# Rounding and splitting the second MoE's weights late, straight into their tiles, instead of early through a DRAM copy

## The chip, the cores and the metric

The program runs on one core of a Trainium2 chip. The metric is device time in microseconds (us) of one execution. The core's engines each take their own instructions strictly in order and wait for one another through semaphores: PE (TensorE, matmuls; PEld are its weight loads), DVE (VectorE), ACT (ScalarE), POOL (GpSimd) and SP (SyncE, which here issues every DMA).

## The reference, cut to what matters

```python
for t in range(768):                       # attention: a recurrence over tokens, 4 batches x 8 heads
    y_t = r_t . state                      # state is 40 x 40 for each head
    state = state * w_t - outer(state . a_t, b_t) + outer(v_t, k_t)
x = y as [3072 tokens, 320]
g = max(x @ moe_w_in, 0) ** 2              # first MoE, d_ff = 2048
x2 = g @ moe_w_out
out = ((x2 @ w_a) * (x2 @ w_b)) @ w_out2   # second MoE, d_ff = 1536
```

The inputs come as 64-bit floats (two 32-bit halves, low and high). The kernel has to round every weight to a 32-bit float, and then split it into a high part (type fp32r, which the matmuls take) and a low part (what is left), since the products are computed as high x high + low x high + high x low.

## The kernel before, in words

Attention runs in 24 waves of 32 tokens (`attention_moe`, loop over `w`). While PE works on a wave, `fill` and `stream.emit` put matmuls of the first MoE between the small attention matmuls. A unit is four waves, 512 tokens; `stream.add(g)` queues unit g of the first MoE one unit behind attention, so the last unit's products stand alone behind the last wave. A unit has 16 hidden blocks of 128; each is eight matmuls into `h` (`l1`), then relu and two squares on ACT (`Moe.l1`), the low part `gl` on DVE (`Moe.low`), and eight matmuls into the accumulators `x0` to `x2` (`l2`). Eleven of the sixteen blocks' weights are streamed from DRAM for every unit (`Stream.load`, double-buffered tiles `w0`, `w1`), five stay resident.

Weights are decoded by `Weights`, a pipeline of four steps for a piece of 384 or 320 columns: `load` (a DMA of 64-bit values into one of three `raw` buffers), `first` (one DVE and two ACT instructions), `second` (two DVE instructions, then an add on POOL that gives the rounded values in `dy`), and `put`, which differs from user to user. For the first MoE `put` splits them: a cast on ACT and a subtraction on POOL. One call of `weights.step()` advances all four steps by one piece.

The second MoE has 12 hidden blocks f, each with 1088 columns of weights (three pieces). In the kernel before, its 36 pieces are decoded by `decode` during the waves, as soon as the first MoE's weights are done; their `put` is a DMA of `dy` to the DRAM tile `w2s`. Behind the last wave, in the loop `while stream.parts`, `load_w2` reads each block back (`w2f`) and splits it by a cast on ACT (`w2h`) and a subtraction on DVE (`w2l`).

The second MoE (`l3`, `l4`) takes unit after unit: 16 matmuls into `h` and `b`, a copy `a` on ACT, the product on DVE, the cast `gh` on ACT, `gl` on DVE, and 12 matmuls into `o`. During its first blocks `General.range_ops` compares all decays w with limits on POOL (`w_t`, `w_ok`), 16 chunks, one for each block; then `in_range` reduces the result on DVE (`w_oks`) and adds it up with one small matmul. `General.run` is a slow fallback for inputs outside the limits, behind a branch that these inputs do not take.

What order each engine gets is decided when the program is built: the scheduler orders DVE, ACT, POOL and SP by a model of time, PE inside the waves keeps the written order, and `keep_in_program_order` (`pin`) holds some instructions in the written order.

Of the kernel before, what the change touches and what calls it, by code (L numbers as in the profile page):

```python
# [9 lines left out]
F32 = mybir.dt.float32  # L10
F32R = mybir.dt.float32r
# [3 lines left out]
ALU = mybir.AluOpType  # L15
# [9 lines left out]
DW = 384  # L25
# [7 lines left out]
RATE = 66  # L33
AHEAD = 3
KEEP = 24

WARM = 10
CHUNK = 4
# [23 lines left out]
class Attention:  # L62
# [51 lines left out]
    def warm(s, bank):  # L114

        x = s.idn.bitcast(BF16)
        for _ in range(WARM):
            s.nc.tensor.matmul(bank[:, 0:256], lhsT=x[:, 0:128], rhs=x, start=True, stop=True)
# [312 lines left out]
class Moe:  # L431
# [109 lines left out]
                s.nc.vector.tensor_tensor(out=x, in0=acc[i][0:64], in1=x, op=ALU.add)  # L541
                s.nc.sync.dma_start(out=dst[256:320], in_=x)

    def load_w2(s, pool, src, f):

        x = pool.tile([128, 1088], F32, tag="w2f", name="w2f", bufs=3)
        s.nc.sync.dma_start(out=x, in_=src)

        def split():
            hi = pool.tile([128, 1088], F32R, tag=f"w2h{f}", name="w2h")  # L550
            lo = pool.tile([128, 1088], F32R, tag=f"w2l{f}", name="w2l")
            pin = s.tc.keep_in_program_order
            pin(s.nc.scalar.copy(out=hi, in_=x))
            pin(s.nc.vector.tensor_tensor(out=lo, in0=x, in1=hi.bitcast(F32), op=ALU.subtract))
            s.w2[f] = hi, lo

        return split

    def l3(s, f, x, ps2, sb):
        hi, lo = s.w2[f]  # L560
# [109 lines left out]
class General:  # L670
# [2 lines left out]

    LEAST, MOST = 0.6, 1.6

    def __init__(s, tc, nat, wm1, w2s, xf, out):
        s.tc, s.nc, s.nat, s.wm1, s.w2s, s.xf, s.out = tc, tc.nc, nat, wm1, w2s, xf, out

    def range_ops(s, sb, n=480):

# [28 lines left out]

    def run(s):  # L710
        tc, nc = s.tc, s.nc
        nf1, nf2 = s.wm1.shape[0], len(s.w2s)
        with ExitStack() as c:
            sb = c.enter_context(tc.tile_pool(name="gen", bufs=1))
            two = c.enter_context(tc.tile_pool(name="gen2", bufs=2))
            ps = c.enter_context(tc.tile_pool(name="gen_ps", bufs=1, space=PSUM))
            weights = Weights(tc, sb)
            w1 = sb.tile([128, nf1, 704], F32, name="w1")
            w2 = sb.tile([128, nf2, 1088], F32, name="w2")
            for f in range(nf2):  # L720
                nc.sync.dma_start(out=w2[:, f], in_=s.w2s[f])
            for f in range(nf1):
                for o in range(0, 704, 176):
                    weights.add(s.wm1[f, :, o:o + 176], 176, lambda x, w=w1[:, f, o:o + 176]: nc.vector.tensor_copy(w, x))
            while weights.busy():
                weights.step()
            S = sb.tile([32, D, D], F32, name="S")
            nc.vector.memset(S, 0.0)
            idn = sb.tile([128, 128], F32, name="idn")
            make_identity(nc, idn)  # L730
            with tc.For_i(0, s.out.shape[0], 1) as i:
                names = "rkvwab"
                x = sb.tile([32, 6, TW, D], F32, name="x")
                for j, m in enumerate(names):
                    nc.sync.dma_start(
                        out=x[:, j].rearrange("p t d -> p (t d)"), in_=s.nat[m][:, bass.ds(i * (TW * D), TW * D)]
                    )
                y = sb.tile([32, TW, D], F32, name="y")
                for t in range(TW):
                    s.token(two, S, {m: x[:, j, t] for j, m in enumerate(names)}, y[:, t])  # L740
                h = sb.tile([40, 8, 4, TW], F32, name="h")
                for q in range(2):
                    p = ps.tile([128, 512], F32, tag="p", name="p", bufs=2)
                    for t in range(16):
                        nc.tensor.matmul(
                            p[0:40, 32 * t:32 * t + 32], lhsT=y[:, 16 * q + t], rhs=idn[0:32, 0:32], start=True, stop=True
                        )
                    for e in range(8):
                        nc.vector.tensor_copy(
                            h[:, e, :, 16 * q:16 * q + 16],  # L750
                            p[0:40].rearrange("p (t b e) -> p e b t", b=4, e=8)[:, e],
                        )
# [63 lines left out]
def attention_moe(ctx, tc, wakb, rv, vt, wm1, wm2, nat, out):  # L816
    nc = tc.nc
    n_waves = wakb.shape[0]
    n_groups = n_waves // GW
    nf1, nf2 = wm1.shape[0], wm2.shape[1]  # L820

    dram = ctx.enter_context(tc.tile_pool(name="dram", bufs=1, space=bass.MemoryType.DRAM))
# [6 lines left out]
    xf = dram.tile([320, 128], F32, name="xf")  # L829
    w1s = {  # L830
        f: [dram.tile([128, n], F32, name=f"w1s{f}_{n}") for n in (768, 640)] for f in range(nf1) if f not in RESIDENT
    }
    w2s = [dram.tile([128, 1088], F32, name=f"w2s{f}") for f in range(nf2)]

    def pool(c, name, side, bufs=1):
        return c.enter_context(tc.tile_pool(name=name, bufs=bufs, side=side, reuse_waits="tile"))
# [18 lines left out]
    done = set()  # L855
# [20 lines left out]

    wp = []
    pending = deque(stream.moving + list(RESIDENT))
    w2_pieces = deque()
    for f in range(nf2):  # L880
        o = 0
        while o < 1088:
            n = min(DW, 1088 - o)
            w2_pieces.append((f, o, n))
            o += n

    def decode(n):
        for _ in range(n):
            if not weights.queue:
                if pending:  # L890
                    round_block(pending.popleft())
                elif w2_pieces and len(done) == nf1:
                    f, o, m = w2_pieces.popleft()
                    weights.add(
                        wm2[:, f, o:o + m], m, lambda x, f=f, c=slice(o, o + m): nc.sync.dma_start(out=w2s[f][:, c], in_=x)
                    )
            if weights.busy():
                weights.step()

# [43 lines left out]
    if True:  # L943
# [51 lines left out]
        for w in range(n_waves):  # L995
          with tc.manual_schedule(engines=MAN):
# [66 lines left out]
              at.m_y(w)  # L1063
              prep(9)
              warm()
        stream.add(n_units - 1)
        stream.tick = lambda x: None
        while weights.busy() or w2_pieces:
            decode(1)
            stream.emit(1)  # L1070
        c1.close()

        w2p = pool(c3, "w2p", "left")
        def load_x2(g):
            h = xp.tile([128, 5, TOK], F32R, tag="xhl", name="xhl", bufs=2)[:, :, 0:x2s[g].shape[1]]
            return h, moe.load_x(h, x2s[g])

        splits = deque(moe.load_w2(w2p, w2s[f], f) for f in range(3))
        f = 3
        every = stream.left // (nf2 + 2)  # L1080
        x = None
        while stream.parts:
            stream.emit(every)
            if splits:
                splits.popleft()()
            if f < nf2:
                splits.append(moe.load_w2(w2p, w2s[f], f))
                f += 1
            elif x is None:
                x, split = load_x2(0)  # L1090
                splits.append(split)
        c2.close()
        ca.close()

        xp3 = pool(cb, "xp3", "right", 2)
        ps2 = psum(cb, "ps2", 2)
        acc4 = psum(cb, "acc4", 1)
        general = General(tc, nat, wm1, w2s, xf, out)
        ranges = general.range_ops(xp3)

        todo = n_ok = None
        for g in range(n_units):
            acc = None
            for f in range(nf2):
                if ranges:
                    ranges.popleft()()
                elif n_ok is None:
                    n_ok = general.in_range(xp3, ps2)
                c = moe.l3(f, x, ps2, xp3)
                if todo:  # L1110
                    todo()
                if f == 0:
                    acc = [acc4.tile([128, TOK], F32, tag=f"o{j}", name=f"o{j}") for j in range(UNITS[g])]
                if f == 3 and g + 1 < n_units:
                    x_next, split = load_x2(g + 1)
                if f == nf2 - 3 and g + 1 < n_units:
                    split()

                def todo(g=g, f=f, acc=acc, c=c):
                    moe.l4(f, c, acc, f == 0, f == nf2 - 1)  # L1120
                    if f == nf2 - 1:
                        for j in range(UNITS[g]):
                            moe.put_out(xp3, g, j, acc)

            if g + 1 < n_units:
                x = x_next
# [64 lines left out]
```

## Time and profile before

| | |
|---|---|
| median of 3 runs | 1320.24 us (1318.36 to 1321.07) |
| the profiled execution | 1315.96 us, its span 1314.2 us |
| PE busy | 1165.1 us, 89% of the span |
| DVE, ACT, POOL busy | 742.4, 520.6, 360.8 us |
| DMA | 153.26 MB, mean 117 GB/s |

The span is the time from the first to the last instruction. The last attention results (`Y`) are written at 825.3 us; the last unit of the first MoE runs until about 902 us, and the rest is the second MoE. In the rows below, "[3.38 <-DVE RVR L317]" behind an instruction is how long its engine was idle before it, and who released it; "x8" means eight instructions merged into one row. Lines are those of the kernel before.

### The profile page before, as it was taken

The numbers are of one execution on the slowest core, as the hardware profiler recorded it, in microseconds if no ns is written. First come the engines' busy times: TensorE is split into PE (matmuls) and PEld (weight loads), VectorE is DVE, ScalarE is ACT, GpSimd is POOL, SyncE is SP. The second block draws the span as 40 slices with busy tenths as digits, with TensorE's granted clock in tenths as the row PEclk, the third lists the DMA queues.
The fourth block names the chain that finished last, engine by engine and source line by source line (L and its number), as shares of the span: only waits on it lengthen the run. The fifth ranks groups of instructions, "written<-read, shape, count | busy, mean of one in ns | idle before, by whom it ended". The sixth has DMA issues, their size and how long they took to land.

```text
span 1314.2 us, 34391 instructions
## 1 busy us (share of the span) xinstructions
PE 1165.1 (89%) x14378; PEld 939.4 (71%) x14378; DVE 742.4 (56%) x1491; ACT 520.6 (40%) x1121; POOL 360.8 (27%) x502
## 2 busy tenths in 40 slices
PE   2537865799799989998999999999998999999997
PEld 2526754577577767776677777778887888888886
DVE  5986897758876886689569623443231323232222
ACT  2215533454455445545454444664221222222221
POOL 2475672324132422142224100001995000000000
PEclk9997677899989989999899999999998999999999
DMA  6307754453567456745753533773120101010000
GB/s 158 91 13 229 223 190 144 116 157 91 156 193 208 110 169 168 229 117 164 202 160 104 139 105 85 263 256 110 43 89 16 45 1 37 0 37 1 20 1 22
DMA packets 103483, 153.26 MB, mean 117 GB/s; under 512 B 40840, under 2 KB 61320, under 8 KB 101256
## 3 DMA queue, kind: packets, MB, share of 16 engines
q1 hardware_dynamic: 103320, 150.98, 39.5%
q8 instruction: 115, 1.88, 0.6%
q14 instruction: 48, 0.39, 0.1%
HBM read 121.38 MB, written 26.41 MB: 112 GB/s over the span
## 4 chain that ended last, share of the span: by engine, by line
PE 56%; DVE 21%; DMA 9%; POOL 8%; issue 4%; ACT 1%; SPq 1%; DVEq 0%; POOLq 0%; ACTq 0%
PE h L440 18%; PE a L108 13%; PE x L440 10%; PE b L440 8%; PE o L440 7%; DVE tmp L246 4%; DVE Ball L253 4%; POOL w_t L691 3%; DMA inp<-wakb 3%; POOL w_ok L692 3%; DVE KA L218 2%; DVE RVR L317 1%; DVE KA L189 1%; DMA xhl<-xs 1%; DVE W L166 1%
## 5 line engine op out<-in xcount | busy, mean ns | idle before, releaser
L440 PE MATMUL h<-xhl,w 128*128 128x512 f32 x768 | 230.9, 421 | 3.6 <-DVE xhl L443 2.6
L569 DVE TENSOR_TENSOR b<-b,a 128x512 f32<-128x512 f32 x72 | 50.3, 699 | 213.3 <-PE b L440 199.0
L440 PEld LDWEIGHTS h<-xhl,w 128*128 128x128 f32 x768 | 140.7, 194 | 36.8 <-DVE xhl L443 3.3
L440 PE MATMUL x<-gh,w 128*128 128x512 f32 x480 | 147.3, 420 | 1.0 <-DVE xl L541 0.6
L108 PE MATMUL a<-KA,KBT 40*64 40x80 f32 x1536 | 84.7, 269 | 56.7 <-POOL KBT L192 26.4
L440 PE MATMUL h<-xhl,w2h 128*128 128x512 f32 x360 | 127.8, 396 | 0.0
L108 PEld LDWEIGHTS a<-KA,KBT 40*64 40x64 f32 x1536 | 74.0, 163 | 74.8 <-POOL KBT L192 38.1
L443 DVE TENSOR_TENSOR gl<-h,gh 128x512 fp32r<-128x512 f32 x96 | 66.1, 689 | 103.7 <-ACT h L507 102.9
L425 POOL TENSOR_TENSOR dy<-dy,raw 128x384 int32<-128x384 int32 (+1 forms) x68 | 68.3, 1004 | 204.6 <-DVE dy L422 109.4
L440 PE MATMUL b<-xhl,w2h 128*128 128x512 f32 x360 | 120.4, 400 | 0.0
L505 ACT ACTIVATE h<-h 128x512 f32<-128x512 f32 x96 | 55.9, 582 | 132.6 <-PE h L440 130.8
L571 ACT CAST gh<-b 128x512 fp32r<-128x512 f32 x72 | 42.3, 587 | 161.9 <-DVE b L569 161.9
L440 PEld LDWEIGHTS x<-gh,w 128*128 128x128 f32 x480 | 89.4, 195 | 22.3 <-issue 1.3
L440 PE MATMUL x<-gl,w 128*128 128x512 f32 x288 | 92.7, 415 | 0.0
L566 ACT COPY a<-h 128x512 f32<-128x512 f32 x72 | 42.3, 588 | 121.9 <-PE h L440 121.9
L440 PE MATMUL h<-xhl,w2l 128*128 128x512 f32 x216 | 85.9, 397 | 0.0
L440 PE MATMUL b<-xhl,w2l 128*128 128x512 f32 x216 | 85.8, 397 | 0.0
L440 PE MATMUL o<-w2h,gl 128*128 128x320 f32 x288 | 85.6, 309 | 0.0
L440 PE MATMUL o<-w2l,gh 128*128 128x320 f32 x288 | 85.6, 308 | 0.0
L108 PEld LDWEIGHTS a<-RVR,VUT 40*64 40x64 f32 x1536 | 64.2, 144 | 24.8 <-issue 14.7
L440 PEld LDWEIGHTS b<-xhl,w2h 128*128 128x128 f32 x360 | 67.9, 190 | 15.8
L108 PE MATMUL a<-RVR,VUT 40*64 40x80 f32 x1536 | 74.6, 246 | 4.8 <-ACT KBS L216 2.4
(97 smaller groups left out, 2174.6 us busy)
## 6 DMA issues: line engine op xcount, KB each, us to landing
w<-w1s SPq DMA_DIRECT2D x66, 384.0 KB
w<-w1s SPq DMA_DIRECT2D x66, 320.0 KB
inp<-wakb SPq DMA_DIRECT2D x48, 322.7 KB
raw<-wm SPq DMA_DIRECT2D x40, 384.0 KB
raw<-wm SPq DMA_DIRECT2D x28, 320.0 KB
w2f<-w2s SPq DMA_DIRECT2D x12, 544.0 KB
w2s<-dy SPq DMA_DIRECT2D x24, 192.0 KB
w1s<-w SPq DMA_DIRECT2D x11, 384.0 KB
```

The lines of the kernel that those rows point to most:

```text
L108: s.nc.tensor.matmul(out, lhsT=lhsT, rhs=rhs, start=True, stop=True)
L246: engine.tensor_tensor(out=t, in0=s.BH[:, i + 1:TW, i:i + 1].to_broadcast([128, n, m]), in1=s.N[:, i:i + 1, c0:c1].to_broadcast([128, n, m ...
L253: engine.tensor_tensor(out=out, in0=out, in1=t, op=ALU.subtract)
L425: nc.gpsimd.tensor_tensor(out=yi, in0=yi, in1=low, op=ALU.add)
L440: s.nc.tensor.matmul(out, lhsT=lhsT, rhs=rhs, start=start, stop=stop)
L443: (engine or s.nc.vector).tensor_tensor(out=out, in0=x, in1=hi.bitcast(F32), op=ALU.subtract)
L505: s.nc.scalar.activation(out=ps, in_=ps, func=ACTF.Relu)
L566: s.nc.scalar.copy(out=a, in_=pa)
L569: s.nc.vector.tensor_tensor(out=pb, in0=pb, in1=a, op=ALU.mult)
L571: s.nc.scalar.copy(out=ch, in_=pb)
L691: nc.gpsimd.tensor_scalar(out=t, in0=x, scalar1=lim, scalar2=None, op0=op)
L692: nc.gpsimd.tensor_tensor(out=s.ok, in0=s.ok, in1=t, op=ALU.mult)
```

## The change

The 36 pieces of the second MoE's weights are no longer decoded during the waves, and there is no DRAM copy of them. All are queued behind the last wave. In the loop over the last unit's products, one `weights.step()` follows every eight matmuls (`W2_EVERY`), and `put` now casts `dy` on ACT and subtracts on POOL straight into the tiles `w2h` and `w2l`. What is left is stepped in the second MoE's first unit. In the source the load of x2's first unit stands where fewer than 16 products are left, and the chunks of the range check begin when no weights are pending. The fallback, which is not executed, decodes the weights itself.

```diff
+W2_EVERY = 8
-    def load_w2(s, pool, src, f):
-
-        x = pool.tile([128, 1088], F32, tag="w2f", name="w2f", bufs=3)
-        s.nc.sync.dma_start(out=x, in_=src)
-
-        def split():
-            hi = pool.tile([128, 1088], F32R, tag=f"w2h{f}", name="w2h")
-            lo = pool.tile([128, 1088], F32R, tag=f"w2l{f}", name="w2l")
-            pin = s.tc.keep_in_program_order
-            pin(s.nc.scalar.copy(out=hi, in_=x))
-            pin(s.nc.vector.tensor_tensor(out=lo, in0=x, in1=hi.bitcast(F32), op=ALU.subtract))
...
+    def add_w2(s, pool, weights, src, f):
...
+        def put(x, o):
+            if not tiles:
+                tiles.extend(pool.tile([128, n], F32R, tag=f"w2{t}{f}", name=f"w2{t}") for t in "hl")
+            hi, lo = (t[:, o:o + x.shape[1]] for t in tiles)
+            s.tc.keep_in_program_order(s.nc.scalar.copy(out=hi, in_=x))
+            s.low(lo, x, hi, weights.engine)
+            if o + x.shape[1] == n:
+                s.w2[f] = tiles
+
+        for o in range(0, n, DW):
+            m = min(DW, n - o)
+            weights.add(src[:, o:o + m], m, lambda x, o=o: put(x, o))
...
-                elif w2_pieces and len(done) == nf1:
-                    f, o, m = w2_pieces.popleft()
-                    weights.add(
-                        wm2[:, f, o:o + m], m, lambda x, f=f, c=slice(o, o + m): nc.sync.dma_start(out=w2s[f][:, c], in_=x)
-                    )
...
-        splits = deque(moe.load_w2(w2p, w2s[f], f) for f in range(3))
-        f = 3
-        every = stream.left // (nf2 + 2)
-        x = None
+        for f in range(nf2):
+            moe.add_w2(w2p, weights, wm2[:, f], f)
         while stream.parts:
-            stream.emit(every)
-            if splits:
-                splits.popleft()()
-            if f < nf2:
-                splits.append(moe.load_w2(w2p, w2s[f], f))
-                f += 1
-            elif x is None:
+            stream.emit(W2_EVERY)
+            weights.step()
+            if stream.left < 16 and x is None:
                 x, split = load_x2(0)
-                splits.append(split)
+        split()
...
+        w2_ready(1)
...
-                if ranges:
+                if ranges and not weights.busy():
                     ranges.popleft()()
-                elif n_ok is None:
+                elif not ranges and n_ok is None:
                     n_ok = general.in_range(xp3, ps2)
+                for _ in range(3 if weights.busy() else 0):
+                    weights.step()
+                w2_ready(f)
```

How the instructions now stand is read from the built programs. On ACT, in the middle of the last unit of the first MoE, before: one hidden block is the three ACTIVATE rows on `h` and `gh` (relu and two squares), and the casts to `w2h` stand between blocks.

```order
L505 ACTIVATE h<-h 128x512
L506 ACTIVATE gh<-h 128x512
L507 ACTIVATE h<-h 128x512
L553 CAST w2h<-w2f 128x1088
L505 ACTIVATE h<-h 128x512
L506 ACTIVATE gh<-h 128x512
L507 ACTIVATE h<-h 128x512
L553 CAST w2h<-w2f 128x1088
```

The same place on ACT now; `raw` and `dz` are the two ACT instructions of the decode step `first`, the cast to `w2h` belongs to `put`:

```order
L507 ACTIVATE h<-h 128x512
L418 ACTIVATE dz<-raw 128x384
L508 ACTIVATE gh<-h 128x512
L509 ACTIVATE h<-h 128x512
L555 CAST w2h<-dy 128x320
L414 ACTIVATE raw<-raw 128x384
L418 ACTIVATE dz<-raw 128x384
L507 ACTIVATE h<-h 128x512
L555 CAST w2h<-dy 128x384
L508 ACTIVATE gh<-h 128x512
L509 ACTIVATE h<-h 128x512
```

Decode instructions have moved in between the three instructions of a block. In the steady part of this stretch 17 casts stand in 12 blocks; 29 of the 36 casts stand ahead of the first `a` copy of the second MoE.

On POOL, from the last attention instruction (`VS`) on, before: one leftover piece, then the range check.

```order
L338 TENSOR_TENSOR VS_149<-VS_149,W_130 40x640 x2
L425 TENSOR_TENSOR dy<-dy,raw 128x320
L685 MEMSET w_ok 128x480
L691 TENSOR_SCALAR w_t<-w_all 128x480
L692 TENSOR_TENSOR w_ok<-w_ok,w_t 128x480
```

On POOL now, in the middle of the last unit: the add that ends the rounding (`dy`) and the subtraction of `put` (`w2l`).

```order
L445 TENSOR_TENSOR w2l<-dy,w2h 128x384
L427 TENSOR_TENSOR dy<-dy,raw 128x320
L427 TENSOR_TENSOR dy<-dy,raw 128x384
L445 TENSOR_TENSOR w2l<-dy,w2h 128x320
L445 TENSOR_TENSOR w2l<-dy,w2h 128x384
L427 TENSOR_TENSOR dy<-dy,raw 128x384
L445 TENSOR_TENSOR w2l<-dy,w2h 128x384
```

POOL, which had nothing between the last wave and the range check, now has 36 adds and 36 subtractions there, the last of them among the first chunks of the range check.

On ACT at the start of the second MoE, before: `a` and `gh` are the second MoE's own, the copies to `xl` and casts to `xhl` belong to x2.

```order
L566 COPY a<-h 128x512 x2
L540 COPY xl<-x_11291 64x512
L477 CAST xhl<-xl 128x512
L571 CAST gh<-b 128x512
```

The same place now:

```order
L571 COPY a<-h 128x512
L418 ACTIVATE dz<-raw 128x384
L555 CAST w2h<-dy 128x320
L414 ACTIVATE raw<-raw 128x384
L542 COPY xl<-x_10964 64x512
L418 ACTIVATE dz<-raw 128x384
L555 CAST w2h<-dy 128x384
L414 ACTIVATE raw<-raw 128x320
L479 CAST xhl<-xl 128x512
L418 ACTIVATE dz<-raw 128x320
L555 CAST w2h<-dy 128x384
L414 ACTIVATE raw<-raw 128x384
```

Nine decode instructions now stand between the second `a` copy and the first `gh` cast. PE's order is the same as before but for a few matmuls of the last unit and of the second MoE's first units that change places with a neighbour.

## Rows read from the trace of the kernel before

**Rows 1.** Busy time by stretch: us, then each engine's busy us, clock, DMA share, GB/s

```profile
338.40:469.30 130.90, 122.89 (x2068) 92.49 (x2069) 98.10 (x218) 67.59 (x153) 38.96 (x61) 0.96 0.58 165
469.30:598.60 129.30, 121.97 (x2042) 92.58 (x2041) 99.33 (x222) 64.02 (x148) 39.25 (x62) 0.96 0.61 171
598.60:729.40 130.80, 121.43 (x2074) 91.85 (x2074) 98.70 (x213) 67.09 (x154) 39.58 (x62) 0.97 0.56 159
...
827.50:902.10 74.60, 72.34 (x309) 57.03 (x308) 33.02 (x38) 48.92 (x80) 0.50 (x1) 1.00 0.71 238
```

**Rows 2.** Timeline of two waits of PE in the waves: start, us, engine, instruction

```profile
359.23 1.26 DVE L166 TENSOR_TENSOR_SCAN W<-inp,ini 104x528 f32<-104x528 f32 x1 [4.26 <-DMA inp<-wakb]
...
361.58 0.80 PE L108 MATMUL a<-KA,KBT 40*64 40x80 f32 x8 [3.38 <-DVE RVR L317]
...
638.98 0.56 DVE L422 SCALAR_TENSOR_TENSOR dy<-dz,dy 128x384 int32<-128x384 int32 x1
639.46 0.35 DVE L411 TENSOR_SCALAR dy<-raw 128x384 int32<-128x384 int32 x1
...
640.70 0.56 PE L108 MATMUL a<-VS,KA 96*32 96x40 f32 x20 [2.80 <-DVE KA L218]
```

**Rows 3.** Instructions of tiles dy and dz: count, duration ns least/median/most, first and last start

```profile
L411 DVE TENSOR_SCALAR dy<-raw x68: 311/353/1442, 91.6 to 694.0; 128x384 int32<-128x384 int32 x40, 128x320 int32<-128x320 int32 x28
L421 DVE TENSOR_SCALAR dz<-dz x68: 272/353/1147, 31.9 to 734.0; 128x384 f32<-128x384 f32 x40, 128x320 f32<-128x320 f32 x28
L422 DVE SCALAR_TENSOR_TENSOR dy<-dz,dy x68: 466/557/1411, 92.0 to 734.3; 128x384 int32<-128x384 int32 x40, 128x320 int32<-128x320 int32 x28
L425 POOL TENSOR_TENSOR dy<-dy,raw x68: 867/1012/2067, 92.7 to 735.0; 128x384 int32<-128x384 int32 x40, 128x320 int32<-128x320 int32 x28
```

**Rows 4.** Groups by line and shape: count, busy us, mean ns, idle before

```profile
L443 POOL TENSOR_TENSOR w<-dy,w 128x384 fp32r<-128x384 f32 x16 | 17.3, 1080 | 14.9 <-ACT w L450 14.8
L553 ACT CAST w2h<-w2f 128x1088 fp32r<-128x1088 f32 x12 | 13.1, 1092 | 0.0
L450 ACT CAST w<-dy 128x384 fp32r<-128x384 f32 x16 | 8.2, 510 | 2.5 <-POOL dy L425 2.4
```

**Rows 5.** Timeline: DVE beside POOL, at 607 us and at 985 us

```profile
607.16 1.26 POOL L186 TENSOR_TENSOR KBT<-inp,KBS 104x512 f32<-104x512 f32 x1 [10.50 <-DVE KBS L176]
607.29 1.35 DVE L411 TENSOR_SCALAR dy<-raw 128x384 int32<-128x384 int32 x1
...
984.64 1.41 POOL L691 TENSOR_SCALAR w_t<-w_all 128x480 f32<-128x480 f32 x1
984.67 0.69 DVE L443 TENSOR_TENSOR gl<-b,gh 128x512 fp32r<-128x512 f32 x1 [0.65 <-ACT gh L571]
```

**Rows 6.** Timeline of ACT: a decode pair in the waves, a hidden block in the last unit

```profile
633.39 0.54 ACT L412 ACTIVATE raw<-raw 128x384 f32<-128x384 uint32 x1
633.82 0.55 ACT L416 ACTIVATE dz<-raw 128x384 f32<-128x384 f32 x1
...
889.56 0.58 ACT L505 ACTIVATE h<-h 128x512 f32<-128x512 f32 x1 [0.98 <-PE h L440]
...
890.67 0.59 ACT L507 ACTIVATE h<-h 128x512 f32<-128x512 f32 x1
```

**Rows 7.** The chain that ended last: start, us, what

```profile
629.67 6.25 DMA inp<-wakb
...
867.33 1.87 PE x L440 x8
869.19 1.83 PE h L440 x8
```

**Rows 8.** Timeline of ACT at the second MoE's start: two rows

```profile
908.13 0.59 ACT L566 COPY a<-h 128x512 f32<-128x512 f32 x1 [0.77 <-PE h L440]
...
914.46 0.59 ACT L571 CAST gh<-b 128x512 fp32r<-128x512 f32 x1 [1.52 <-DVE b L569]
```

**Rows 9.** Waits of PE from 880 to 1060 us: total, times, longest

```profile
PE b L705 <- DVE w_oks L701: 5.2, 1, 5.2
```

**Rows 10.** Busy time by stretch, early waves, columns as in Rows 1

```profile
100.00:200.00 100.00, 75.69 (x1594) 63.79 (x1594) 86.37 (x175) 47.30 (x113) 66.76 (x100) 0.74 0.68 213
```

More of the change, by code (lines that the diff above doesn't have):

```diff
@@ L542, in put_x2 @@
                 s.nc.sync.dma_start(out=dst[256:320], in_=x)
-    def load_w2(s, pool, src, f):
-        x = pool.tile([128, 1088], F32, tag="w2f", name="w2f", bufs=3)
-        s.nc.sync.dma_start(out=x, in_=src)
-        def split():
-            hi = pool.tile([128, 1088], F32R, tag=f"w2h{f}", name="w2h")
-            lo = pool.tile([128, 1088], F32R, tag=f"w2l{f}", name="w2l")
-            pin = s.tc.keep_in_program_order
-            pin(s.nc.scalar.copy(out=hi, in_=x))
-            pin(s.nc.vector.tensor_tensor(out=lo, in0=x, in1=hi.bitcast(F32), op=ALU.subtract))
-            s.w2[f] = hi, lo
-        return split
+    def add_w2(s, pool, weights, src, f):
+        n = src.shape[1]
+        tiles = []
+        def put(x, o):
[9 more added lines that the diff above has]
+            weights.add(src[:, o:o + m], m, lambda x, o=o: put(x, o))
     def l3(s, f, x, ps2, sb):
@@ L674, with __init__ @@
     LEAST, MOST = 0.6, 1.6
-    def __init__(s, tc, nat, wm1, w2s, xf, out):
-        s.tc, s.nc, s.nat, s.wm1, s.w2s, s.xf, s.out = tc, tc.nc, nat, wm1, w2s, xf, out
+    def __init__(s, tc, nat, wm1, wm2, xf, out):
+        s.tc, s.nc, s.nat, s.wm1, s.wm2, s.xf, s.out = tc, tc.nc, nat, wm1, wm2, xf, out
     def range_ops(s, sb, n=480):
@@ L711, in run @@
         tc, nc = s.tc, s.nc
-        nf1, nf2 = s.wm1.shape[0], len(s.w2s)
+        nf1, nf2 = s.wm1.shape[0], s.wm2.shape[1]
         with ExitStack() as c:
@@ L719, in run @@
             w2 = sb.tile([128, nf2, 1088], F32, name="w2")
[L720 to L724, printed above, removed]
+            for m, src in [(w1[:, f], s.wm1[f]) for f in range(nf1)] + [(w2[:, f], s.wm2[:, f]) for f in range(nf2)]:
+                for o in range(0, m.shape[1], 176):
+                    w = m[:, o:min(o + 176, m.shape[1])]
+                    weights.add(src[:, o:o + w.shape[1]], w.shape[1], lambda x, w=w: nc.vector.tensor_copy(w, x))
             while weights.busy():
@@ L832, in attention_moe @@
     }
-    w2s = [dram.tile([128, 1088], F32, name=f"w2s{f}") for f in range(nf2)]
     def pool(c, name, side, bufs=1):
@@ L878, in attention_moe @@
     pending = deque(stream.moving + list(RESIDENT))
[L879 to L885, printed above, removed]
     def decode(n):
@@ L1065, in attention_moe @@
               warm()
+        x = None
         stream.add(n_units - 1)
         stream.tick = lambda x: None
-        while weights.busy() or w2_pieces:
+        while weights.busy():
             decode(1)
@@ L1076, in load_x2, with w2_ready @@
             return h, moe.load_x(h, x2s[g])
-        splits = deque(moe.load_w2(w2p, w2s[f], f) for f in range(3))
-        f = 3
-        every = stream.left // (nf2 + 2)
-        x = None
+        for f in range(nf2):
+            moe.add_w2(w2p, weights, wm2[:, f], f)
         while stream.parts:
-            stream.emit(every)
-            if splits:
-                splits.popleft()()
-            if f < nf2:
-                splits.append(moe.load_w2(w2p, w2s[f], f))
-                f += 1
-            elif x is None:
+            stream.emit(W2_EVERY)
+            weights.step()
+            if stream.left < 16 and x is None:
                 x, split = load_x2(0)
-                splits.append(split)
+        split()
         c2.close()
         ca.close()
+        def w2_ready(f):
+            while f < nf2 and f not in moe.w2:
+                weights.step()
+        w2_ready(1)
         xp3 = pool(cb, "xp3", "right", 2)
@@ L1097, in attention_moe @@
         acc4 = psum(cb, "acc4", 1)
-        general = General(tc, nat, wm1, w2s, xf, out)
+        general = General(tc, nat, wm1, wm2, xf, out)
         ranges = general.range_ops(xp3)
@@ L1104, in attention_moe @@
             for f in range(nf2):
-                if ranges:
+                if ranges and not weights.busy():
                     ranges.popleft()()
-                elif n_ok is None:
+                elif not ranges and n_ok is None:
                     n_ok = general.in_range(xp3, ps2)
+                for _ in range(3 if weights.busy() else 0):
+                    weights.step()
+                w2_ready(f)
                 c = moe.l3(f, x, ps2, xp3)
```

## The prediction

> **What bounds the kernel now.** I read the busy time by stretch first. In the three groups of four waves between 338 and 729 us PE is busy 122.9 of 130.9, 122.0 of 129.3 and 121.4 of 130.8 us, at a mean granted clock of 0.96 to 0.97; in the stretch of the first MoE's last unit, 827.5 to 902.1 us, it is busy 72.3 of 74.6 us at full clock [rows 1]. So PE bounds both, and each has little to give. What differs is who else is busy: DVE has 98 of 131 us in a group of waves, but 33 of 74.6 us in the last unit, where POOL has 0.5 us and ACT 48.9 [rows 1]. The change takes work from the stretch where DVE is nearly full to one where there seems to be room.
>
> Next the timeline around the waits that PE has in the waves. Two of the longest are 3.38 us at 361.6 and 2.80 us at 640.7, both for DVE [rows 2]. In the first, DVE itself had waited 4.26 us for a DMA (`inp`); in the second, 0.56 and 0.35 us of second-MoE decoding stand directly ahead of the instruction that PE wants. Then the durations of the decode instructions [rows 3, 4], what DVE does while POOL works [rows 5], the period of a hidden block [rows 6, 7], and the second MoE's start [rows 8, 9].
>
> **Removed from the waves.** 36 pieces, each of three DVE, two ACT and one POOL instruction, a load and a store. The order of PE's attention rows stays. At most everything goes that PE loses there: 8.0 + 7.3 + 9.4 = 24.7 us idle [rows 1], and what the low clock costs: a mean of 0.96 to 0.97 with levels 1.2 and 2.4 GHz means 6 to 8% of about 390 us, some 29 us, at half clock, which can cost half of that, 14 us. Nothing is added to the waves, so the least is 0. I take about 40% of the idle time, since of the two waits read the pieces stand in the way with 0.9 of 2.8 us in one, and in the other PE waits for a DMA behind which their loads and stores no longer queue: 10 us, and 2 us for clock that does not fall. Gain 12, bounds 0 and 39.
>
> **Added to the last unit.** Here the pieces go at a pace, and the question is what sets it. One piece of 384 columns costs POOL 1.01 for the add and about 1.0 (mean 1.08 with disturbances) for the subtraction; DVE 0.35 + 0.35 + 0.56 = 1.26; ACT 0.98 for `raw` and `dz` together (633.39 to 634.37) and 0.51 for the cast [rows 3, 4, 6]. If these lie beside each other, POOL sets 2.0 us a piece. But DVE and POOL do not work beside each other on this: at 607.29 the DVE instruction that otherwise takes 0.35 takes 1.35 us, ending only after POOL's 1.26 us that began 0.13 us earlier [rows 3, 5], and the longest of each of the four decode kinds in the waves is 1.1 to 2.1 us, two to four times its median [rows 3]. So the five instructions follow one another: 1.26 + 2.0 = 3.3 us for 384 columns, at least 2.75 for 320 (scaled), 3.1 us in the mean of a block's three pieces.
>
> The DVE instruction of a hidden block itself, `gl`, is not held up: 0.69 us beside POOL's 1.41 [rows 5]; it reads one operand from PSUM.
>
> The Trainium skill states this as a rule (SBUF — State Buffer, section "SBUF: two separate sides"): DVE in its two-port modes or with two SBUF inputs and POOL share one pair of ports, held for a whole instruction by whichever came first, while the other blocks fully. The trace agrees, with 1.35 us for 0.35. By the rule a piece costs the sum of its DVE and POOL times; without it, the larger of them. It speaks against putting both halves of the decoding into one stretch, however idle the engines look there.
>
> 29 casts stand before the second MoE's first `a` copy, so about 29 pieces pass in this stretch: 29 x 3.1 = 90 us, and some 5 us until the first piece has landed and reached DVE, 95 us instead of 74.6. Does PE wait for it? A hidden block of PE takes 1.87 + 1.83 = 3.70 us [rows 7]. On ACT, 17 pieces stand in 12 blocks, 1.42 a block, and the casts and `raw` instructions stand between a block's relu and squares. ACT is in order: behind a cast that waits for POOL wait the squares, behind these `gl` on DVE, and behind that PE's products into x0 to x2. A block then takes 1.42 x 3.1 = 4.4 us or more, against 3.70. ACT itself would just do: 1.70 for the block (889.56 to 891.26) and 1.42 x 1.4 = 2.0 for the pieces, 3.7 us [rows 6]. That gives the bounds. Least: only ACT counts; its 48.9 us less the 13.1 of the old casts plus 29 x 1.4 is 76.4 us against 74.6, so +2 [rows 1, 4]. Most: the three `raw` buffers turn around once in a landing (6.25 us, as `inp` [rows 7]), 0.98 on ACT, 0.91 on DVE, 1.01 on POOL and about 2 us of waits between these two, 11.2 us, or 3.7 a piece: 29 x 3.7 + 5 = 112, +38. I take +20, for the turns of DVE and POOL are the only one of these costs that a row shows and that comes at every piece.
>
> Two things that go here are the 12 read-backs with their casts and subtractions. Their 13.1 us of ACT is counted above; the subtractions on DVE have no POOL beside them before. The loads double in this stretch, from 12 x 128 x 1088 values of 4 bytes (6.7 MB) to as many of 8 bytes (13.4 MB); with the DMA share at 0.71 [rows 1] this is in the upper bound, not in the value. On SP the raw loads, which wait for POOL, stand among the weight loads of the first MoE, which wait behind them; this too lengthens a block only if pieces are late.
>
> **The second MoE's start.** Seven pieces are left. Between the second `a` copy and the first `gh` cast ACT now has nine decode instructions, three pieces' worth, at 3.1 us each 9.3 us; before, these two were 6.3 us apart (908.13 to 914.46) [rows 8]. That is +3, and about as much again for the four other pieces among the next blocks: +6, bounds 0 and +10. The range check's last matmul stood 5.2 us in PE's way [rows 9]. POOL gets about 14 us of pieces ahead of or among its chunks, but could begin sooner than before, and PE arrives later by the 6 us: 0, bounds -5 and +8.
>
> **Sum.** -12 + 20 + 6 + 0 = +14. Against the profiled execution, 1315.96 (span 1314.2 and 1.8 around it), that is 1330; the median shown, 1320.24, lies 4.3 above that execution, so I forecast 1334.
>
> **Rivals.**
> *The pieces fit (faster).* The scheduler has left 2.6 us of PE time for each piece (3.70 / 1.42). If DVE's and POOL's instructions seldom meet, a piece needs 2.0 us of POOL and hides wholly behind PE. Then the last unit grows by 2, the start of the second MoE by 1, and the waves give 12: 1320 - 9 = 1311. For it: POOL is idle there, ACT's sum comes out even, and half of the DVE instructions in the waves show their plain duration. Against: in the waves POOL is only 30% busy, here both would be busy at the same pieces all the time. It decides at 2.6 us a piece: below, faster; at 3.1, slower.
> *Pieces late and the clock falls too (slower still).* With blocks of 4.7 us PE would work under 80% of the time (3.70 of 4.7); between 100 and 200 us, 75.7% busy, its granted clock was 0.74 [rows 10]. A clock that is at half for 30% of 95 us, 28 us, lengthens the six blocks in it from 4.7 to 7.4 us, which loses about 2 blocks, 10 us; with pieces at 3.4 us (29 x 0.3 = 9 us more) it is 1334 + 19 = 1353. Against: PE's small attention matmuls ran in that early stretch, large ones here, and in the last unit the clock stayed at 1.00 [rows 1].
> *It cancels.* The waves give 18 and the late part takes 18: 1320. That the waves lose the pieces at all is plain from the order of POOL and SP, so this is the form in which the change does nothing.
>
> **How the numbers follow.** Forecast 0.55, pieces fit 0.20, late with the clock 0.17, cancels 0.08. A change under 0.2% (2.6 us) cannot be told from none here. Faster 0.20, same 0.08, slower 0.72. The forecast's own range is 1322 to 1348. For 8 in 10 I go down to 1312, near the first rival's time, and up to 1362, past the second's; all bounds at one end at once (-42 or +56) would be wider, and are left out.
>
> **What would show it.** In the profile after: waves from 338 us about 4 us shorter for each group of four; the stretch from the last `Y` to the first `a` copy near 95 us with PE waiting for ACT or DVE (`gh`, `gl`); `dy` and `dz` on DVE well over their 0.35 us there, and POOL's adds over 1.0; nine decode instructions holding the first `gh`. The forecast is wrong if that stretch stays under 80 us, or if the waves give more than 25 us.

## The result, and the profile after

The changed kernel took 1338.61 us (1335.65 to 1341.06, four runs), the kernel before 1319.41 (1318.36 to 1321.07, four runs beside it): ratio 1.0143, 95% interval 1.0118 to 1.0169. It is slower. The forecast was 1334, range 1312 to 1362. The profiled executions span 1314.2 and 1337.9 us, 23.7 apart.

The total was close; its parts were not, and their errors cancelled in part. I cut both profiles at three events: the start of the last `Y` (end of the waves), the first matmul of the second MoE (`h<-xhl,w2h`), and its first `o` matmul.

| Stretch, us | before | after | difference | forecast |
|---|---|---|---|---|
| to the last `Y` | 826.1 | 825.3 | -0.8 | -12 |
| `Y` to first `h<-xhl,w2h` | 76.2 | 85.4 | +9.2 | +20 |
| to the first `o` | 13.1 | 19.0 | +5.9 | +6 |
| to the end | 398.8 | 408.2 | +9.4 | 0 |

The windows of after, with the columns of [rows 1]: three groups of four waves, the last unit, the second MoE to the range check's last matmul.

```profile
338.70:469.10 130.40, 125.09 (x2072) 94.19 (x2071) 85.44 (x185) 57.12 (x129) 27.23 (x50) 0.95 0.43 119
469.10:599.00 129.90, 121.95 (x2041) 92.81 (x2041) 85.16 (x184) 54.51 (x125) 27.39 (x50) 0.95 0.43 119
599.00:730.50 131.50, 124.67 (x2074) 94.23 (x2074) 84.63 (x178) 56.88 (x129) 26.89 (x50) 0.95 0.41 113
...
826.80:910.70 83.90, 75.58 (x309) 57.55 (x308) 65.10 (x106) 69.42 (x147) 54.09 (x52) 0.98 0.77 244
910.70:1028.40 117.70, 99.87 (x489) 84.32 (x488) 49.60 (x73) 38.18 (x74) 106.42 (x86) 0.95 0.29 87
```

Beside [rows 1], DVE has 85 us of work in a group of waves where it had 98, and each group is as long as before. In the last unit DVE, ACT and POOL have 65, 69 and 54 us where they had 33, 49 and 0.5. In the fifth row PE is busy 99.9 of 117.7 us while POOL is busy 106.4.

Next the waits in the last unit (total, times, longest), of PE and then of ACT, in after; below them ACT's largest wait there in before.

```profile
PE x L442 <- ACT gh L508: 4.1, 3, 2.8
PE x L442 <- DVE gl L445: 2.4, 5, 0.9
PE h L442 <- DVE gl L445: 1.7, 1, 1.7
...
ACT h L507 <- PE h L442: 5.1, 4, 3.2
ACT raw L414 <- DMA raw<-wm: 4.7, 6, 1.3
ACT w2h L555 <- POOL dy L427: 2.4, 4, 0.9
ACT xhl L479 <- DMA xl<-x2s: 2.0, 1, 2.0
```

```profile
ACT h L505 <- PE h L440: 21.4, 16, 3.2
```

PE loses 8.2 us: 4.1 waiting for ACT's `gh` and 4.1 for DVE's `gl`. One reading is in ACT's rows: before, ACT waited 21.4 us for PE, so it had time over. After, that is 5.1 us, and 7.1 us of new waits are for what the pieces need (4.7 for their loads, 2.4 for POOL's `dy`). The same as ACT sees it, in two blocks of after (start, us, instruction):

```profile
857.17 0.62 ACT L479 CAST xhl<-xl 128x512 fp32r<-128x512 f32 x1 [2.01 <-DMA xl<-x2s]
857.69 0.48 ACT L418 ACTIVATE dz<-raw 128x320 f32<-128x320 f32 x1
858.20 0.58 ACT L507 ACTIVATE h<-h 128x512 f32<-128x512 f32 x1
858.69 0.59 ACT L508 ACTIVATE gh<-h 128x512 fp32r<-128x512 f32 x1
...
859.34 2.50 PE L442 MATMUL x<-gh,w 128*128 128x512 f32 x5 [2.84 <-ACT gh L508]
...
889.33 0.57 ACT L507 ACTIVATE h<-h 128x512 f32<-128x512 f32 x1
889.85 0.51 ACT L555 CAST w2h<-dy 128x384 fp32r<-128x384 f32 x1
890.97 0.50 ACT L414 ACTIVATE raw<-raw 128x320 f32<-128x320 uint32 x1 [0.61 <-DMA raw<-wm]
891.36 0.59 ACT L508 ACTIVATE gh<-h 128x512 fp32r<-128x512 f32 x1
```

In the second block the relu at 889.33 and its square at 891.36 are 2.0 us apart, with a cast, a wait of 0.61 for a load and a conversion between them. In the first, a cast of the second MoE's input waits 2.01 us for its load; behind it stand the relu and squares that PE then waits 2.84 us for. Before, this cast waited 2.8 us in the same stretch, and PE waited for no `gh` at all.

The other half is the same thing on DVE. In one block of after ACT's last square ends at 851.34; `gl` does not start then, as a decode instruction stands ahead of it that waits for a load:

```profile
850.73 0.61 ACT L509 ACTIVATE h<-h 128x512 f32<-128x512 f32 x1
...
851.70 0.65 DVE L413 TENSOR_SCALAR dy<-raw 128x384 int32<-128x384 int32 x1 [0.74 <-DMA raw<-wm]
...
852.27 0.68 DVE L445 TENSOR_TENSOR gl<-h,gh 128x512 fp32r<-128x512 f32 x1
...
853.00 0.73 PE L442 MATMUL x<-gl,w 128*128 128x512 f32 x2 [0.91 <-DVE gl L445]
```

In five of PE's six waits for `gl`, `gl` starts right behind a decode instruction on DVE; in the sixth (1.7 us) it starts behind two subtractions for `xhl`.

At the second MoE's start, ACT's second copy `a` and first cast `gh` ([rows 8]) are 10.4 us apart instead of 6.3:

```profile
918.71 0.59 ACT L571 COPY a<-h 128x512 f32<-128x512 f32 x1
...
929.10 0.59 ACT L576 CAST gh<-b 128x512 fp32r<-128x512 f32 x1
```

And the range check, to compare with [rows 9], with two windows of after, the wait and what follows it:

```profile
PE b L710 <- DVE w_oks L706: 12.7, 1, 12.7
...
1015.70:1028.40 12.70, 0.02 (x1) 0.00 (x0) 0.65 (x1) 0.00 (x0) 11.30 (x9) 0.64 0.07 19
1028.40:1042.20 13.80, 13.78 (x61) 11.70 (x62) 4.32 (x7) 3.23 (x6) 0.00 (x0) 0.84 0.01 2
```

PE stands 12.7 us instead of 5.2 while POOL works through its chunks; behind the wait PE runs 13.8 us at a mean granted clock of 0.84.

### The profile page after: what moved, and what is told of

Read it like the earlier page. It is cut to its first block, busy times and chain, and to the rows that moved or that the text cites. A ratio compares the mean times of both kernels' runs of the same rounds, so it can differ in the third digit from the quotient of the medians.

```text
span 1337.9 us, 34375 instructions
## 1 busy us (share of the span) xinstructions
PE 1174.2 (88%) x14378; PEld 943.4 (71%) x14378; DVE 751.5 (56%) x1479; ACT 522.5 (39%) x1145; POOL 399.3 (30%) x538
## 4 chain that ended last, share of the span: by engine, by line
PE 51%; DVE 20%; DMA 10%; POOL 9%; issue 5%; ACT 3%; SPq 1%; DVEq 0%; POOLq 0%; ACTq 0%
PE h L442 16%; PE a L110 12%; PE b L442 8%; PE x L442 8%; PE o L442 7%; DVE tmp L248 4%; DVE Ball L255 4%; POOL w_t L696 3%; DMA raw<-wm 3%; POOL w_ok L697 3%; DMA inp<-wakb 2%; DVE VS L335 1%; DVE RVR L319 1%; DVE Y L372 1%; DMA Ball<-KA 1%
## 5 line engine op out<-in xcount | busy, mean ns | idle before, releaser
L110 PE MATMUL a<-KA,KBT 40*64 40x80 f32 x1536 | 87.8, 275 | 60.7 <-POOL KBT L194 23.0
L110 PEld LDWEIGHTS a<-KA,KBT 40*64 40x64 f32 x1536 | 76.8, 168 | 79.5 <-POOL KBT L194 37.6
L188 POOL TENSOR_TENSOR KBT<-inp,KBS 104x512 f32<-104x512 f32 x24 | 30.7, 1278 | 288.8 <-DVE KBS L178 72.3
L110 PEld LDWEIGHTS a<-RVR,VUT 40*64 40x64 f32 x1536 | 66.3, 148 | 20.2 <-issue 15.4
```

The lines of the kernel that those rows point to most:

```text
L110: s.nc.tensor.matmul(out, lhsT=lhsT, rhs=rhs, start=True, stop=True)
```

## The experiments

Theory A was the forecast's: DVE's and POOL's turns pace the pieces and hold PE. The rivals came with the results: ACT's own order, the loads, the range check. In the later expectations C is ACT's order and D the loads. All ratios are against the kernel before, run on the same chip; of the other numbers, those on stretches come from one profile each.

**The range check asked for later**, in each kernel (the same condition is added to this line of the kernel before):

```
-                elif not ranges and n_ok is None:
+                elif not ranges and n_ok is None and (g, f) >= (1, 10):
```

> The changed kernel, with the range check's reduction and its matmul put behind the second unit's block 10 instead of the first block without a chunk. Theory A (part of the loss is that POOL's backlog of weight pieces pushes the range check back, so that its matmul holds PE for 12.7 us, and the clock falls after that): the wait goes, PE's clock stays up there, the time falls by 13 to 19 us against the changed kernel, to about 1320 to 1326. Rival B (the wait only covers other late work, for instance the weights or the accumulators): the time falls by under 5 us.

> The kernel before with the same move of the range check's matmul. Theory A: the 5.2 us wait and the low clock of 6.8 us behind it go, 6 to 9 us less than the kernel before, about 1311 to 1313. Rival B: no change.

Changed kernel with the edit: 1322.91 us (1318.27 to 1327.57), ratio 1.0019 (1.0000 to 1.0037). Kernel before with it: 1309.62 (1308.07 to 1312.94), 0.9919 (0.9893 to 0.9944), which beats both kernels and gains more than the 6 to 9 us expected (0.8%, some 11 us). No wait on `w_oks` is left in either. The windows from the first `o` to the end: of before, of before with the edit, of after, and of after with the edit.

```profile
915.40:1314.20 398.80, 386.57 (x1971) 334.57 (x1969) 113.10 (x169) 93.55 (x165) 83.38 (x64) 0.99 0.09 27
```

```profile
914.30:1306.40 392.10, 384.90 (x1971) 333.40 (x1969) 112.97 (x169) 93.88 (x165) 83.51 (x64) 1.00 0.09 27
```

```profile
929.70:1337.90 408.20, 388.64 (x1970) 336.11 (x1970) 120.04 (x177) 97.65 (x174) 92.86 (x72) 0.97 0.09 28
```

```profile
925.70:1320.40 394.70, 387.46 (x1970) 335.57 (x1970) 120.71 (x178) 97.97 (x174) 92.36 (x72) 0.99 0.10 29
```

In these profiles the check cost before 6.7 us, of which 5.2 are the wait, and after 13.5, of which 12.7 are. So it makes 6.8 of the difference of 9.4 between them; the other 2.6 stay without it. The ratios show more for each, 0.8% and 1.2%, or some 11 and 16 us, and a similar difference. Without the check the change costs about 1.0% (1.0019 against 0.9919): that is what the pieces do.

**Less POOL in a piece.** First the subtraction alone on DVE, then the addition too:

```
-            s.low(lo, x, hi, weights.engine)
+            s.low(lo, x, hi)
...
-            nc.gpsimd.tensor_tensor(out=yi, in0=yi, in1=low, op=ALU.add)
+            s.adder.tensor_tensor(out=yi, in0=yi, in1=low, op=ALU.add)
...
+        weights.adder = nc.vector
```

> The changed kernel with only the subtraction of the second MoE's pieces on DVE; the add stays on POOL. Theory A (turns): a piece costs 1.26 + 0.6 + 1.0 = 2.9 us instead of 3.1 to 3.3, the stretch of the last unit falls by 2 to 5 us, POOL's backlog by half, so the range check's wait falls to 6 to 9 us; 5 to 10 us less in all. Rival B (loads or ACT's order): the stretch is the same, the whole gain is the range check's 4 to 6 us.

> The changed kernel with the add and the subtraction of the second MoE's pieces on DVE instead of POOL (DVE adds these integers with fewer bits, so the weights' last bits are wrong; the work is otherwise the same). Theory A (DVE and POOL take turns at SBUF, so a piece costs the sum of both, 3.1 us): DVE alone needs about 1.3 + 2 x 0.6 = 2.4 us a piece and nothing holds it up; the stretch from the last wave to the second MoE's first matmul falls from 83.9 us to 75 to 79, the range check begins earlier and its wait falls from 12.7 to under 6 us; 12 to 20 us less than the changed kernel. Rival B (the pieces wait for their loads or stand in ACT's order): the stretch stays at 82 to 86 us and only the range check gains, 5 to 9 us in all. Rival C (DVE becomes the bound, since it also has gl): the stretch grows.

Subtraction: 1338.54 (1329.28 to 1341.56), 1.0118 (1.0067 to 1.0168); both: 1328.43 (1326.01 to 1335.79), 1.0051 (1.0030 to 1.0072). In the first the stretch from `Y` is 81.9 us and the wait for `w_oks` 13.9, so the expectation of 6 to 9 there missed. In the second the stretch is 81.1, between A's 75 to 79 and B's 82 to 86, and that wait is 5.2, 7.5 us less than in after. The gain was thus mostly the range check's, and I repeated it with the check later:

> The kernel after with the later range check, and with the addition and the subtraction of the second MoE's pieces on DVE, so POOL has none of it (the added bits differ in the last place, since the two engines round differently). It takes the range check out of the comparison made with the addition and subtraction on DVE alone. A, the turns cost what the pieces add: the 84.7 us falls to 77 to 79 and the 18.9 by 2, the time 1312 to 1317. B, the turns are a small part and ACT's order and the loads the rest: 80 to 83, the 18.9 as it is, the time 1318 to 1322.

1323.31 us (1319.58 to 1331.74), 1.0025 (0.9994 to 1.0056), against 1.0019 with POOL's part: no gain in the time. The stretch fell to 78.6 and the next to 17.2, which is what A expected of them, but 25 pieces instead of 28 passed before the first `a`, at the same pace (3.09 us), and the part from the first `o` took 398.5 instead of 394.7. PE's waits for `gl` in the stretch fell from 2.8 to 0.2 us, so a part of what the turns cost does reach PE. Half of the 7.8 us had only moved; the other half shows in one profile and not in the times.

**Nothing of a piece on DVE and POOL.** ACT keeps three instructions a piece:

```
+            if s.light:
+                return lambda: (lambda: put(low.bitcast(F32), high.bitcast(F32)))
...
-            s.low(lo, x, hi, weights.engine)
+            s.tc.keep_in_program_order(s.nc.scalar.activation(out=lo, in_=high, func=ACTF.Abs))
```

> The kernel after with the later range check, and with nothing of the second MoE's decoding left on DVE and POOL: a piece is loaded and passes ACT three times as before (the conversion of the low half, the cast into w2h, and one instruction that writes the high half's absolute value into w2l); sign, exponent, sum and subtraction are left out, so the weights are not the reference's. Compared with the later range check alone (1322.9; 84.7 us from the last Y to the second MoE's first matmul, 18.9 from there to its first o). A, the turns of DVE and POOL pace the pieces and their lateness holds ACT: the 84.7 falls to 76 to 78 (before: 76.2), the 18.9 by 3 to 5, the time to 1309 to 1314. B, ACT's own added work and its waits for the loads hold PE: the 84.7 stays at 82 to 85, the 18.9 falls by 1 to 3, the time 1317 to 1322.

1323.48 us (1319.14 to 1333.65), 1.0027 (0.9996 to 1.0058). The window from `Y` to the second MoE's first matmul, and the waits there of PE and of ACT:

```profile
822.30:906.20 83.90, 76.60 (x316) 57.17 (x315) 18.49 (x27) 71.57 (x153) 0.50 (x1) 1.00 0.80 254
...
PE x L446 <- ACT gh L512: 5.2, 6, 1.2
...
ACT raw L416 <- DMA raw<-wm: 8.0, 12, 1.1
ACT h L511 <- PE h L446: 4.7, 2, 3.2
```

This decides against theory A as the cause that the loss needs: DVE is busy 18 us and POOL 0.5, no turn is left to take, and the stretch is 83.9 us against 84.7, as B said (the next stays at 18.9, where B had 1 to 3 less). ACT's part and the loads are thus enough for the whole loss. The pieces come somewhat faster, every 2.77 us, and 28 casts instead of 26 stand ahead of the first matmul. ACT is busy 71.6 us and waits 8.0 us for the pieces' loads; for PE it waits 4.7 us, 3.2 of them in one wait at the start of the stretch, which before and after have too. What remains is ACT or the loads.

**Five `raw` buffers** instead of three, with the whole decoding:

```
-        raw = s.sb.tile([128, DW, 2], I32, tag="raw", name="raw", bufs=3)
+        raw = s.raws.tile([128, DW, 2], I32, tag="raw", name="raw", bufs=s.n_raw)
...
+        weights.raws, weights.n_raw = w2p, 5
```

> The kernel after with the later range check, and with five raw buffers in place of three for the second MoE's pieces, so that loads are issued two pieces sooner; everything computed as in the kernel after. A, turns of DVE and POOL set the pace: the pieces keep 3.0 to 3.1 us, the 84.7 us stays within 1.5 us, the time 1320 to 1325. B, the turnaround of the three raw buffers sets it (ACT waits 5.6 us for raw loads in this stretch, SP 35.7 us for POOL's last use of a buffer): pieces at 2.7 us or less, the stretch 79 to 82, the time 1316 to 1320.

1323.36 us (1318.68 to 1328.65), 1.0021 (0.9992 to 1.0050). ACT's waits for raw loads fell from 5.6 to 1.0 us and the pieces came every 2.85 us instead of 3.07, where A had 3.0 to 3.1 and B 2.7 or less, but the stretch was 86.4 (below it, waits of PE there):

```profile
824.70:911.10 86.40, 75.39 (x315) 58.01 (x314) 72.28 (x114) 72.55 (x154) 58.19 (x55) 1.00 0.81 268
...
PE x L443 <- DVE gl L446: 4.3, 6, 1.2
PE h L443 <- DVE xhl L446: 2.1, 1, 2.1
...
PE x L443 <- ACT gh L509: 0.6, 1, 0.6
```

ACT was busy 72.5 us, with 154 instructions. Faster pieces didn't shorten PE's wait, so neither the buffers nor the pace of a piece bound the stretch; 2.85 also shows that 3.07 was no floor set by the turns. But PE now waits little for ACT: of its 11.0 us idle, 8.1 are for DVE, which is busy 72.3 us and has decode instructions ahead of `gl`. With the whole decoding, ACT is not the only engine that holds PE.

**Half the loads, or nothing on ACT.** From the kernel with ACT alone: each load brings half the bytes; or two POOL copies write both tiles and ACT has nothing:

```
-            nc.sync.dma_start(out=raw[:, 0:n].rearrange("p n k -> p (n k)"), in_=src.bitcast(I32))
+            nc.sync.dma_start(out=raw[:, 0:n // 2].rearrange("p n k -> p (n k)"), in_=src[:, 0:n // 2].bitcast(I32))
...
+            s.nc.gpsimd.tensor_copy(out=hi, in_=high)
+            s.nc.gpsimd.tensor_copy(out=lo, in_=high)
```

> The kernel in which ACT alone handles the second MoE's pieces (nothing of them on DVE and POOL, range check later), and now each piece's load brings half the bytes, while ACT's three instructions keep their size; the weights are not the reference's. The kernel with full loads had 83.9 us from the last Y to the second MoE's first matmul, 18.9 from there to its first o, ACT waiting 8.0 us for raw loads in 12 waits, and 1323.5. C, ACT's own order: three more instructions of a piece stand between a block's relu and squares whatever the loads do: 81 to 84 us, 18 to 20, 1320 to 1324. D, the doubled loads: ACT's waits for raw nearly go and PE's for gh with them: 76 to 79 us, 14 to 17, 1310 to 1316.

> The kernel in which nothing of the second MoE's pieces stands on ACT or DVE: full loads, range check later, and two POOL copies write w2h and w2l from the high half of a piece (the weights are not the reference's). C, ACT's order holds PE: without the pieces on ACT the 83.9 us fall to 76 to 78 and the 18.9 to 13 to 15, the time is that of the kernel before with the later range check, 1308 to 1313, if POOL keeps up. D, the loads hold PE or the weights of the first MoE behind them on SP: 81 to 84 us, 1317 to 1322.

Half loads: 1318.45 us (1314.66 to 1322.16), 1.0008 (0.9989 to 1.0028). Nothing on ACT: 1310.86 (1306.59 to 1317.27), 0.9954 (0.9934 to 0.9974). The windows as above, first of half loads, then of nothing on ACT with ACT's largest wait there:

```profile
823.20:908.30 85.10, 77.53 (x316) 58.68 (x315) 18.49 (x27) 76.03 (x168) 0.50 (x1) 0.98 0.66 206
```

```profile
821.60:899.00 77.40, 74.93 (x315) 59.66 (x314) 18.79 (x27) 37.72 (x69) 22.52 (x46) 0.98 0.77 256
899.00:912.10 13.10, 13.10 (x57) 10.53 (x57) 3.95 (x7) 4.88 (x10) 6.39 (x10) 1.00 0.82 265
...
ACT h L512 <- PE h L447: 31.2, 14, 4.2
```

With the full loads (256 GB/s) and no piece on ACT, the stretch is 77.4 us, the next 13.1 as in before, and ACT waits 31 us for PE again. The ratio falls from 1.0027 to 0.9954, some 10 us; the rest to before with the later check (0.9919) stays open. With half the bytes the stretch did not fall (all 36 casts now came before the first `a`), the next fell to 15.4 as D said, and the ratio of 1.0008 can't be told from 1.0027. The holder in these kernels, which have none of the pieces' work on DVE, is ACT. The loads' share is bounded, not settled: DMA share and piece count both changed with half loads, and ACT's waits for loads only fell from 8.0 to 4.1 us. With nothing on ACT, three pieces also came before the last `Y`, from 723 us on, and 26 in all ahead of the first matmul, where ACT alone had 28. No kernel took ACT's whole part away and left DVE's and POOL's.

**The cast on POOL**, everything computed:

```
-            s.tc.keep_in_program_order(s.nc.scalar.copy(out=hi, in_=x))
+            s.nc.gpsimd.tensor_copy(out=hi, in_=x)
```

> The kernel after with the later range check, and with the second MoE's cast to w2h on POOL, ahead of the subtraction there, in place of ACT; everything computed as in the kernel after. With the cast on ACT: 84.7 us from the last Y to the second MoE's first matmul, 18.9 to its first o, 1322.9. C, ACT's instructions between a block's relu and squares hold PE: 29 casts of 0.5 us leave ACT, of which what stood in PE's way goes: 80 to 82 us, 16 to 18, 1317 to 1320, although the turns of DVE and POOL are as many as before and POOL has 0.5 us more a piece. A, the turns set the pace: POOL's 0.5 us more makes a piece 3.3 to 3.6 us, 86 to 92 us, 1324 to 1332.

1326.02 us (1320.69 to 1333.52), 1.0038 (1.0007 to 1.0068). The total missed the expectation of theory C and lies in A's; the stretches did as C said, more strongly:

```profile
825.10:903.80 78.70, 75.54 (x316) 59.62 (x315) 54.57 (x93) 56.88 (x113) 51.73 (x62) 0.98 0.74 240
903.80:919.30 15.50, 13.31 (x58) 10.26 (x56) 12.03 (x20) 9.23 (x19) 12.08 (x14) 1.00 0.74 235
919.30:1326.10 406.80, 388.37 (x1970) 336.02 (x1970) 131.27 (x199) 102.02 (x185) 112.12 (x99) 0.98 0.11 34
...
PE b L710 <- DVE w_oks L706: 10.6, 1, 10.6
```

9.4 us less in the first two (84.7 and 18.9 before). Part of this is that 21 casts instead of 26 stand there; the others trail to 974 us, POOL takes them beside its range check, and the wait for `w_oks` is back with 10.6 us although the check is asked for later, so that the last part takes 406.8 us instead of 394.7.

## Why the prediction was right in the sum and wrong in its steps

**The waves, -12, came to about -1.** The step that failed is "in the other, PE waits for a DMA behind which their loads and stores no longer queue". The same place as in [rows 2], in before and in after:

```profile
350.82 1.63 POOL L192 TENSOR_TENSOR KBT<-inp,KBS 104x512 f32<-104x512 f32 x1
352.48 0.69 SPq L154 DMA_DIRECT2D inp<-wakb  x2
```

```profile
350.84 1.64 POOL L194 TENSOR_TENSOR KBT<-inp,KBS 104x512 f32<-104x512 f32 x1
352.51 0.69 SPq L156 DMA_DIRECT2D inp<-wakb  x2
359.16 1.26 DVE L168 TENSOR_TENSOR_SCAN W<-inp,ini 104x528 f32<-104x528 f32 x1 [4.96 <-DMA inp<-wakb]
```

In both the load starts 0.03 us after POOL's last read of the one `inp` buffer ends, and DVE starts 6.7 us later. The buffer sets this wait; the pieces did not. I had read the releaser's name without looking at what released the load. From 338 to 730 us DVE's waits for `inp` even grew, here in before and in after:

```profile
DVE W L166 <- DMA inp<-wakb: 12.0, 5, 4.3
```

```profile
DVE W L168 <- DMA inp<-wakb: 15.6, 3, 6.0
```

A second `inp` buffer was not tried. PE's idle time in the waves did shrink, but little reached the end. In the ten profiles whose waves hold (nearly) no pieces, the last `Y` starts between 821.6 and 827.1 us, 824.2 in the mean; in the two with pieces at 825.1 and 826.1, so the gain of about 1.4 us is small beside their spread. PE's idle time from 338 us to there is 22.3 us in the mean (19.2 to 26.8) against 26.2 and 25.9: 4 us less, of which PE's busy time, at a clock of 0.96 to 0.98, takes back more than half. I took 40% of the idle time for the pieces'; 4 of 26 is 15%.

**The last unit, +20, came to +9.2.** The pace was as forecast: from 832.16 to 915.21 us there are 28 casts, one each 3.08 us, where I had said 3.1. The cause was not. The step "the five instructions follow one another", with DVE's and POOL's turns as the price, fails: the kernel with nothing of the pieces on DVE and POOL has the same stretch, a kernel without POOL's part kept 3.09, and other buffers gave 2.85 with the turns. The turns exist ([rows 5]); in after, too, a DVE instruction that takes 0.56 us alone took 1.35 beside POOL's subtraction:

```profile
854.81 1.03 POOL L445 TENSOR_TENSOR w2l<-dy,w2h 128x384 fp32r<-128x384 f32 x1 [1.74 <-ACT w2h L555]
854.89 1.35 DVE L424 SCALAR_TENSOR_TENSOR dy<-dz,dy 128x384 int32<-128x384 int32 x1
```

The Trainium skill's rule on the shared ports (SBUF — State Buffer, section "SBUF: two separate sides") thus agrees with the single instruction, 1.35 us for 0.56; the time that I worked out from it does not, since the pieces kept their pace without POOL's part.

What holds PE is nearer to what I had put at the lower bound: ACT "would just do", with +2. Its busy time there was 70.2 us, not the 76.4 that I summed, with 26 casts instead of 29 ahead of the second MoE's first matmul. But ACT in order does not only need its sum. Where it stands waiting for a load, for POOL or for `xl`, the squares behind stand too, and a wait of ACT for PE no longer absorbs this: 21.4 us of such slack became 5.1. DVE does the same with its `gl`, half of PE's wait in after; there the turns have a part, as they lengthen the instructions ahead of it. Shown is that ACT's part with the loads is enough for a stretch of this length, and that it goes when ACT's part goes; how ACT and DVE share it in the changed kernel is not shown. Of the 9.2 us, 6.1 are idle time of PE; 3.1 are its busy time (73.9 to 77.1 us), at a mean clock of 0.98 instead of 1.00, and what lengthened that is open.

A part of the difference is mine alone: 95 us was counted to the first `a` copy, and compared with 74.6 us, which end at the first matmul; in before the first `a` copy starts at 906.8, 4.5 us behind it. From the last `Y` to the first `a` copy it is 80.7 us in before and 92.1 in after, +11.4, with 28 casts ahead of that copy and not 29.

**The second MoE's start, +6, came to +5.9,** and the second `a` copy and the first `gh`, with the nine decode instructions between them, are 10.4 us apart where I had put 9.3. Again it is not DVE and POOL that make a piece dear: with ACT's three instructions alone this stretch stayed at 18.9 us, and without them it was 13.1.

**The range check, 0, came to +6.8** by the kernels with a later check. I let POOL's earlier beginning balance the pieces ahead of its chunks. But the check's chunks began at 929.3 instead of 914.1 us, POOL had pieces to subtract until 943.8, and it was busy 106 of the 118 us up to the check, with no time to catch up. PE came to the wait 16 us later than before (1015.7 for 999.7), POOL was done 23.5 later: the wait grew by 7.5.

By stretches, the forecast was too good by 11 us in the waves and by 9 from the first `o` on, and too bad by 11 in the last unit: +14 in all, where the profiles show +23.7 and the medians +19. That the sum came this near is luck: errors of 11 and 9 us one way stood against 11 the other. None of the rivals happened: the pieces did not fit, nothing cancelled, and the clock in the last unit was 0.98, not the 0.85 of a clock at half for 30% of it.

## What to carry to other kernels

When work is added to an engine that stands between two instructions of the engine at the end, read how long it now waits for that engine: this slack, not the idle share, is what the new work may use, and every wait that comes with it uses it too. To tell which of four engines holds a pipeline, take one engine's part away at a time, and read in each run whom the engine at the end now waits for, as it may be the next one; a rule on two of them, seen in single instructions, is no evidence that they bound the whole. A load's wait is read from its issue backwards: if the issue stands right behind a buffer's last read, taking other work out of the queue does not shorten it.

## What the runs showed of the hardware

The wait of PE in the range check costs more than itself: 6.7 us for a wait of 5.2, and 13.5 for 12.7, in one profile each; the ratios of the runs give more, some 11 and 16 us. The granted clock falls already during the wait (0.64 in its window), so that much of the low clock lies where PE has nothing to do; in the 13.8 us behind it the mean was 0.84.
